# A fused retention and two-layer network kernel: V loads on SyncE's queue, each held for another load, and units 4 and 5 attended one by one

## The chip, the core and the metric

The kernel runs on one core of one Trainium2 chip. The metric is the device time of one execution in microseconds (us). The core has five engines with a queue each: PE (TensorE: matmuls, and PEld, its weight loads), DVE (VectorE), ACT (ScalarE), POOL (GpSimd) and SP (SyncE, which here only issues transfers). Transfers are issued by POOL, SP or ACT and carried out by 16 DMA engines that all of them share.

## The reference

Shapes: q, k and v are 8 x 8 x 576 x 64 (batch, heads, positions, head size). The first part is a retention with a decay per head, the second a two-layer network with a gated activation over 4608 tokens of 512 features:

```python
scores = scale * np.matmul(q, k.transpose(0, 1, 3, 2))
gamma = 1.0 - 2.0 ** (-5.0 - np.arange(H, dtype=np.float32))
Dmat = np.where(rel >= 0, gamma[:, None, None] ** rel[None, :, :], 0.0)
ret = np.matmul(scores * Dmat[None, :, :, :], v)
x = ret.transpose(0, 2, 1, 3).reshape(B * S, H * D)
h = x @ w_in                       # 512 -> 2048
g = h * (1.0 / (1.0 + np.exp(-1.702 * h)))
out = g @ w_out                    # 2048 -> 512
```

## The kernel before

**Tiles.** The 4608 tokens are 36 units of 128; four units are a chunk, so there are 9 chunks. A unit's attention ("scores", "values", "inter", "state" in the code) is made of matmuls of 64 x 64 blocks: `scores` (L632) multiplies K and Q, `scores_out` (L641, DVE) masks the result out of PSUM, `state_both` (L561) or `state_half` (L538) multiplies K and V to the running state, `state_sum` (L574, L576, DVE) adds it up, `state_cast` (L585, ACT) writes it as bf16 into `kv`, `values` (L654) multiplies masked scores and V, `inter` (L616) multiplies Q and the state before, and `x_out` or `x_out_pair` (L669, L679, DVE) takes the sum, scaled by the powers of gamma, to `xT`. V is first scaled to `vp` by `scale_v`: on DVE (L480) for units 0 to 7, on ACT (L476, eight instructions of 128x64 per unit) for units 8 to 13, on POOL (L480) for the others.

**The network.** The up projection of a chunk has 16 f tiles of 128 columns of w_in: `up` (L691) makes one f tile for all four units, `up_group` (L705) some f tiles for some of the units; each is followed by one GELU on ACT (L696, L710). From chunk 2 on, `UpSet` (L938, with L949, L953, L962) does the same with fewer products. The down projection is `Pair.run` (L815): seven products of 16 matmuls each, into PSUM banks A and B by turns, copied out by ACT (L828) or added by DVE (L831) into `osb`, and stored.

**Order.** `lead_in()` does units 0 to 3 one by one with parts of chunk 0's up projection, and with dummy matmuls (L1067, L1074) between. `chunk01()` (turn "early") does units 4 to 7, the f tiles 8 to 15 of chunk 0, chunk 1's up projection, and chunk 0's down projection. Units 4 and 5, and 6 and 7, are pairs there: `ahead(j)` gives scores and state of both units of pair j in one go, `block(j)` their values, inter and x. `steady()` runs chunk 1 (turn "first") to chunk 8. In its chunk 1, `hook(1)` calls `ahead(4)`: scores and states of units 8 and 9, between the second and the third product. So PE reaches that third product only when unit 8 and 9 have their scaled V and their transposes.

**Queues.** PE, POOL and SP execute in program order. ACT's and DVE's order is given by a table, PLACES: each operation of a stage has a number there, and the engine executes by 10000 times the turn plus that number, in order, waiting at each for what it needs. PADS gives, for each gap between stages or blocks, how many nops go into PE's instruction stream, one ahead of each of the next matmuls.

**Loads.** K and Q of unit u go to slot u % 12 of `kqn` (L352, L339, cast to bf16 on the way), V to slot u % 10 of `vn` (L365, kept in fp32); both by `load(u)`, all from POOL. Only K and Q of unit 0 are loaded by SP (L372), as fp32 into `osb`, and cast by DVE (L383). The order of POOL's queue in the lead-in: V0, unit 1, unit 2, w_in tiles 0 to 3 (two f tiles per `load_win`, each two DMAs, L387), unit 3, w_in 4 to 7, units 4 and 5, w_in 8 to 15, units 6 and 7, the four quarters of w_out (L394), units 8 and 9, then in `chunk01()` units 10 to 13. Units 0 to 7 are transposed on PE (L496, L491) and copied by ACT or DVE (L509, L512); units from 8 on by transposing DMAs from SP (`dma_transpose`, L526), the first of which waits for V of unit 13. Loads of units 14 to 17 wait for the transpose of unit 13 (`after`), those of later rounds for the transpose of the last unit of the round before. Chunk 0's outputs are stored from ACT's queue, the others from SP's.

Of the kernel before, what the change touches and what calls it, by code (L numbers as in the profile page):

```python
# [30 lines left out]
class Program:  # L31
# [121 lines left out]
    def emit(self, eng, handle, sems):  # L153
# [14 lines left out]


PLACES = {  # L170
    ("early", "dve"): (
# [4 lines left out]
    ),  # L176
    ("early", "act"): (
# [6 lines left out]
    ),  # L184
    ("first", "dve"): (
        -3094, -3087, -161, -1167, -3020, -1459, -1864, -375, -70, 0, 0, -35, 234, -24, 654, 1489, 1403,
        1276, 1426, 1691, 1817, 1256, 1747, 1826, 2319, 1955, 1955, 2266, 2319, 2279, 2367, 1889, 1921, 1958,
        2189, 2222, 2248,
    ),
    ("first", "act"): (  # L190
        89, 1405, 1317, 1538, 1564, 11282, 2193,
    ),
    ("second", "act"): (
        -7652, -7562, -5268, -5221, -6814, -6753, -5520, -5411, -4470, -3949, -4823, -1529, -4083, -3955,
        -1425, -2133, -3938, -3629, -2846, -2700, -1058, 1018, 139, 454, 1345, 2980, 1691, 2832, 13658, 4556,
    ),
    ("second", "dve"): (
# [3 lines left out]
    ),  # L201
    ("mid", "act"): (
        -5145, -5020, -1896, -1729, -4845, -3773, -3705, -1971, -1157, -678, -1349, 2396, -821, -802, 1635,
        2396, -223, 242, 412, 620, 2648, 2953, 2569, 2779, 3397, 4347, 3659, 3701, 13327, 4401,
    ),
    ("mid", "dve"): (
# [3 lines left out]
    ),  # L210
    ("last", "act"): (
        -5412, -4735, -4294, -4481, -4735, -4526, -4516, -4482, -4119, -3957, -4192, -2867, -4110, -4084,
        -2730, -2620, -3883, -3811, -3643, -3308, -2314, -1667, -2542, -1448, -1260, 3388, 5040, 7770, 5228,
        5609, 7636, 11553, 17449, 24766,
    ),
    ("last", "dve"): (
        -4089, -4052, -3782, -3778, -3506, -3367, -3219, -3202, -3136, -3108, -3104, -1962, -1838, -64, -245,
        5700, 171, 274, 5929, 7966, 3319, 9533, 11095, 16923, 5403, 9389, 20259, 16639, 2882, 7994, 13880,
        17309, 21551, 26523,
    ),  # L220
}
# [42 lines left out]
def bass_retnet_parallel__then__act_gelu_quick_kernel(  # L264
# [10 lines left out]
    with es:  # L275
# [93 lines left out]

        def load_kq0(which):  # L370
            src = (k, q)[which]
# [645 lines left out]
        def ahead(j):  # L1017
            if 2 * j < NU:
# [64 lines left out]
        def lead_in():  # L1083
            load_kq0(0)
            load_kq0(1)
            iota_small()
            iota_large()
            load_v(0)
            load(1)
            load(2)  # L1090
            load_win(0, 2)
            load_win(2, 2)
            load(3)
            load_win(4, 2)
# [12 lines left out]
            warm_quads(NQUAD)  # L1107
            warm(44, "A", 64)
# [70 lines left out]
            gq_next(5)  # L1179

        def chunk01():
            scale_v(4)
            transposes(4, "E", "D")
            transposes(5, "C", "K")
            scale_v(5)
            up(0, 8)
            ahead(2)
            now(ahead_out(2))
            for f in range(9, 12):
                up(0, f)  # L1190
            now(block(2, lambda: up(0, 12)))
            up(0, 13)
            for i in range(4):
                up_group(1, 2 * i, 2, 0, 2, "AB"[i % 2])
                if i == 1:
                    transposes(6, "E", "D")
                    scale_v(6)
            transposes(7, "C", "K")
            scale_v(7)
            up_group(1, 8, 2, 0, 2, "A")  # L1200
            ahead(3)
            now(ahead_out(3))
            up_group(1, 10, 2, 0, 2, "B")
            up(0, 14)
            up(0, 15)
            now(block(3, lambda: up_group(1, 12, 2, 0, 2, "A")))
            up_group(1, 14, 2, 0, 2, "B")
# [147 lines left out]
```

## Time and profile before

| what | us |
|---|---|
| median of 3 timed runs | 285.7 (285.69, 285.7, 289.03) |
| the profiled execution | 283.09 |
| its span in the trace | 281.3 |
| PE busy | 267.8 |
| DVE busy | 214.2 |
| ACT busy | 176.5 |
| POOL busy, of which until 50.8 us nearly without a gap | 135.3 |
| software (POOL) transfers, 22.82 MB, as a share of the 16 DMA engines' span | 71.9% |
| hardware (SP and ACT) transfers, 16.00 MB | 25.8% |
| lead-in: transposes of unit 4 start on PE | 24.7 |
| chunk 0's first down product starts on PE | 53.4 |
| chunk 1's third down product starts on PE | 71.8 |
| chunk 2's up projection starts on PE | 83.2 |

The stages overlap, since each engine has its own queue. The span is what the trace covers; the execution's own time is 1.8 us longer. Granted clock: 1.00 throughout. "Busy" of PE counts a matmul until its modelled end, so a small gap between two starts can be invisible in it; in this text a gap of PE is the time between two starts less what the same kind of matmul takes in an unbroken run.

### The profile page before, as it was taken

The numbers are of one execution on the slowest core, as the hardware profiler recorded it, in microseconds if no ns is written. First come the engines' busy times: TensorE is split into PE (matmuls) and PEld (weight loads), VectorE is DVE, ScalarE is ACT, GpSimd is POOL, SyncE is SP. The second block draws the span as 40 slices with busy tenths as digits, with TensorE's granted clock in tenths as the row PEclk, the third lists the DMA queues.
The fourth block names the chain that finished last, engine by engine and source line by source line (L and its number), as shares of the span: only waits on it lengthen the run. The fifth ranks groups of instructions, "written<-read, shape, count | busy, mean of one in ns | idle before, by whom it ended". The sixth has DMA issues, their size and how long they took to land.

```text
span 281.3 us, 10016 instructions
## 1 busy us (share of the span) xinstructions
PE 267.8 (95%) x4402; PEld 220.2 (78%) x4402; DVE 214.2 (76%) x418; ACT 176.5 (63%) x345; POOL 135.3 (48%) x167
## 2 busy tenths in 40 slices
PE   8898999999899999999999999998999999999895
PEld 6576487888688687878887888787878887888584
DVE  5764747878799699669886987796869887966671
ACT  7557675679527952894289428950894289428922
POOL 9999999200297249607755915680572020000000
PEclk9999999999999999999999999999999999999999
DMA  9999999989499979999998999894886070011013
GB/s 170 176 204 210 214 208 210 220 125 268 75 165 133 218 109 180 181 198 106 184 270 100 160 147 213 101 200 81 252 105 76 31 199 0 6 75 76 0 40 112
DMA packets 118027, 40.75 MB, mean 145 GB/s; under 512 B 104160, under 2 KB 111328, under 8 KB 117984
## 3 DMA queue, kind: packets, MB, share of 16 engines
q0 software_dynamic: 80800, 22.82, 71.9%
q1 hardware_dynamic: 36320, 16.00, 25.8%
q10 hardware_dynamic: 864, 1.31, 1.5%
q8 instruction: 34, 0.56, 0.8%
q14 instruction: 9, 0.07, 0.1%
HBM read 36.70 MB, written 9.44 MB: 164 GB/s over the span
## 4 chain that ended last, share of the span: by engine, by line
PE 65%; POOL 16%; ACT 8%; DMA 4%; DVE 3%; issue 2%; ACTq 0%; POOLq 0%
PE psB L815 18%; PE psA L815 14%; POOL kqn L352 7%; DMA vn<-in_v_dram 4%; POOL vn L365 4%; PE psA L938 4%; PE psK L938 4%; PE psX L938 4%; PE psC L938 4%; POOL w_in_sb L387 4%; ACT vp L476 3%; PE psE L938 3%; PE psD L938 3%; PE psY L938 3%; PE psB L938 3%; ACT gT L962 2%
## 5 line engine op out<-in xcount | busy, mean ns | idle before, releaser
L352 POOL DMA_DIRECT2D kqn<-in_k_dram x39 | 36.2, 936 | 49.8 <-DMA kqT<-kqn 49.8
L962 ACT ACTIVATE gT<-part 128x512 bf16<-128x512 f32 (+1 forms) x56 | 47.9, 878 | 0.6 <-DVE part L953 0.5
L828 ACT ACTIVATE osb<-psB 128x512 f32<-128x512 f32 (+1 forms) x25 | 14.7, 589 | 50.2 <-PE psB L815 50.2
L480 POOL TENSOR_TENSOR vp<-vn,vfac 128x512 bf16<-128x512 f32 x22 | 22.5, 1050 | 42.5 <-PE psD L938 35.4
L365 POOL DMA_DIRECT2D vn<-in_v_dram x40 | 37.9, 961 | 0.1
L352 POOL DMA_DIRECT2D kqn<-in_q_dram x37 | 34.4, 941 | 0.0
L815 PE MATMUL psB<-w_out_sb,gT 128*128 128x256 bf16 x224 | 27.0, 273 | 0.0
L815 PEld LDWEIGHTS psB<-w_out_sb,gT 128*128 128x128 bf16 x224 | 21.4, 98 | 4.2 <-DVE part L953 1.9
L585 ACT ACTIVATE kv<-stm 128x1024 bf16<-128x1024 f32 (+1 forms) x16 | 15.5, 970 | 4.3 <-DVE stm L576 4.3
L815 PE MATMUL psA<-w_out_sb,gT 128*128 128x256 bf16 x136 | 16.5, 273 | 1.2 <-ACT gT L962 1.2
L815 PE MATMUL psA<-wsum,part 128*128 128x256 bf16 x136 | 16.3, 273 | 1.4 <-ACT osb L828 1.4
L641 DVE TENSOR_TENSOR pm<-psC,mask 128x512 bf16<-128x512 f32 (+1 forms) x20 | 12.6, 632 | 5.8 <-PE psC L632 5.0
L815 PE MATMUL psB<-wsum,part 128*128 128x256 bf16 x136 | 16.4, 273 | 0.0
L815 PE MATMUL psA<-w_out_sb,part 128*128 128x256 bf16 x120 | 14.8, 273 | 1.5 <-issue 1.5
L815 PEld LDWEIGHTS psA<-wsum,part 128*128 128x128 bf16 x136 | 13.2, 98 | 3.0 <-ACT osb L828 1.5
L953 DVE TENSOR_TENSOR part<-psB,part 128x512 f32<-128x512 f32 x14 | 9.6, 686 | 7.8 <-ACT part L949 7.8
L815 PEld LDWEIGHTS psA<-w_out_sb,gT 128*128 128x128 bf16 x136 | 13.1, 98 | 3.0 <-ACT gT L962 1.5
L641 DVE TENSOR_TENSOR pm<-psD,mask 128x512 bf16<-128x512 f32 (+1 forms) x20 | 12.6, 631 | 3.7 <-PE psD L632 3.7
L679 DVE TENSOR_TENSOR xT<-psX,gq 128x512 bf16<-128x512 f32 x16 | 11.0, 686 | 5.2 <-PE psY L616 5.2
L815 PEld LDWEIGHTS psB<-wsum,part 128*128 128x128 bf16 x136 | 12.7, 98 | 1.9 <-issue 0.2
L476 ACT ACTIVATE vp<-vn,vfac 128x64 bf16<-128x64 f32 x48 | 12.5, 341 | 2.5 <-DMA vn<-in_v_dram 1.9
L815 PEld LDWEIGHTS psA<-w_out_sb,part 128*128 128x128 bf16 x120 | 11.2, 98 | 3.4 <-issue 1.9
(233 smaller groups left out, 772.0 us busy)
## 6 DMA issues: line engine op xcount, KB each, us to landing
vn<-in_v_dram POOLq DMA_DIRECT2D x32, 256.0 KB, 5.9
out_dram<-osb SPq DMA_DIRECT2D x26, 256.0 KB, 2.5
kqn<-in_k_dram POOLq DMA_DIRECT2D x31, 128.0 KB, 5.7
kqn<-in_q_dram POOLq DMA_DIRECT2D x31, 128.0 KB, 5.8
w_in_sb<-in_moe_w_in_dram POOLq DMA_DIRECT2D x16, 128.0 KB, 5.6
w_out_sb<-in_moe_w_out_dram POOLq DMA_DIRECT2D x4, 512.0 KB, 11.3
out_dram<-osb SPq DMA_DIRECT2D x10, 128.0 KB, 2.4
vn<-in_v_dram POOLq DMA_DIRECT2D x8, 128.0 KB, 7.0
```

Source lines behind the costliest of these rows:

```text
L352: e.dma_start(kqn[sl][p0 : p0 + n, which, :, :], src[b, :, s0 : s0 + n, :].rearrange("h p d -> p h d"),)
L365: e.dma_start(vn[sl][p0 : p0 + n, :, :], v[b, :, s0 : s0 + n, :].rearrange("h p d -> p h d"))
L387: op("pool", lambda e: [e.dma_start(w_in_sb[64 * pb : 64 * pb + 64, :, P * f0 : P * f0 + P * nf], moe_w_in[256 * pb : 256 * pb + 256, P * ...
L476: op("act", lambda e, h=h: e.activation(vp[u % NVP][:, h, :], vn[sl][:, h, :], AF.Copy, scale=vfac[:, ty, h : h + 1]), reads=[f"vn{sl}"] + ...
L480: op(eng, lambda e: e.tensor_tensor(vp[u % NVP].ap(), vn[sl].ap(), vfac[:, ty, :, None].to_broadcast([P, H, DH]), ALU.mult), reads=[f"vn{s ...
L585: op("act", lambda e: e.activation(kv[:, i0 % NKV : i0 % NKV + n, :, :], stm[:, i0 % 8 : i0 % 8 + n, :, :], AF.Copy), reads=[f"stm{(i0 + i ...
L641: op("dve", lambda e: e.tensor_tensor(pm[(u0 // 2) % 2][hh][:, c0:c1].rearrange("p (a i) -> p a i", i=64), ps32(SB[hh])[:, c0:c1].rearrang ...
L679: op("dve", lambda e: e.tensor_tensor(xT[ch % 2][:, slice(hh, 4, 2), P * jj : P * jj + 2 * P].rearrange("p g (u t) -> p u g t", u=2), ps32 ...
L815: op("pe", lambda e, x=x, y=y, t=t, s=not more and t == 0 and k == 0, z=k == NF // 2 - 1: e.matmul(bank[b][:, 256 * t : 256 * t + 256], x, ...
L828: op("act", lambda e: e.activation(dst[0], src[0], AF.Copy), reads=src[1], writes=dst[1])
L938: op("pe", lambda e, x=x, y=y, i=i, s=not more and i == 0 and k == 0, z=k == 1: e.matmul(bank[b][:, 256 * i : 256 * i + 256], x, y, start= ...
L962: op("act", lambda e: e.activation(dst, src, AF.Gelu_apprx_sigmoid), reads=reads, writes=[g_key(self.c, f0 + 2 * i + q, j) for i in range( ...
```

## The change

1. `load_v` issues from SP instead of POOL (all units), and in the first stages it is told to wait for another load: V0 and V1 for none, V2 for Q of unit 1, V3 for Q of unit 2, V4 for w_in tile 8, V5 for w_in tile 12, V6 for K of unit 5, V7 for K of unit 6, V8 for quarter 2 of w_out, V9 for K of unit 8, V10 to V13 for K of the unit before. Later V loads wait for the same transpose as before.
2. POOL's order in the lead-in: units 1 and 2, w_in 0 to 3, unit 3, w_in 4 to 11, unit 4, w_in 12 to 15, units 5 to 7, w_out, units 8 and 9 (K and Q alone).
3. Units 4 and 5 are done by a new `single(u)`, one at a time among the f tiles 8 to 15, instead of by `ahead(2)`; `block(2)` stays, with f tile 15 in its middle. Transposes of units 6 and 7 move ahead of chunk 1's up projection, whose groups are spread anew around `ahead(3)` and `block(3)`.
4. PLACES is on a scale ten times finer, with other numbers in every row, and so other orders on ACT and DVE; PADS has other numbers (574 nops for 324).

```diff
-        return 10000 * self.turn + (10 * n if row is None else row[n]), (self.turn, self.kind, n)
+        return 100000 * self.turn + (100 * n if row is None else row[n]), (self.turn, self.kind, n)
...
-    0, 0, 0, 0, 0, 0, 0, 24, 0, 0, 0, 30, 6, 0, 0, 78, 0, 0, 108, 0, 0, 78, 0, 0, 0,
+    0, 0, 92, 0, 0, 16, 16, 0, 0, 114, 0, 0, 99, 0, 0, 81, 0, 0, 104, 0, 0, 52, 0, 0, 0,
...
-        def load_v(u, after=(), eng="pool"):
+        def load_v(u, after=(), eng="sp"):
...
-            op(eng, f, reads=after, writes=[f"vn{sl}"], dma=f"d_vn{sl}_{eng}", ndma=len(unit_rows(u)))
+            op(eng, f, reads=after, writes=[f"vn{sl}"], dma=f"d_vn{sl}", ndma=len(unit_rows(u)))
...
+        def single(u):
+            pr.wide = False
+            scores(u)
+            state_both(u)
+            pr.wide = True
+            for hh in range(2):
+                scores_out(u, 1, hh)
+            for a in range(2):
+                state_sum(u, a)
...
+        def kq(u):
+            load_kq(u, 0)
+            load_kq(u, 1)
...
             load_kq0(0)
             load_kq0(1)
+            load_v(0)
+            load_v(1)
             iota_small()
             iota_large()
-            load_v(0)
-            load(1)
-            load(2)
+            kq(1)
+            kq(2)
+            load_v(2, after=["kq1_1"])
             load_win(0, 2)
             load_win(2, 2)
-            load(3)
-            load_win(4, 2)
-            load_win(6, 2)
-            load(4)
-            load(5)
-            for f in range(8, NF, 2):
+            load_v(3, after=["kq2_1"])
+            kq(3)
+            for f in (4, 6, 8, 10):
                 load_win(f, 2)
-            load(6)
-            load(7)
+            load_v(4, after=["win8"])
+            kq(4)
+            load_win(12, 2)
+            load_win(14, 2)
+            load_v(5, after=["win12"])
+            kq(5)
+            load_v(6, after=["kq5_0"])
+            kq(6)
+            load_v(7, after=["kq6_0"])
+            kq(7)
             for i in range(4):
                 load_wout(i)
             for u in range(8, 10):
-                load(u)
+                load_v(u, after=["wout2" if u == 8 else "kq8_0"])
+                kq(u)
...
         def chunk01():
+            up(0, 8)
+            up(0, 9)
+            transposes(4, "E", "D")
             scale_v(4)
-            transposes(4, "E", "D")
-            transposes(5, "C", "K")
+            up(0, 10)
+            single(4)
+            up(0, 11)
+            up(0, 12)
+            transposes(5, "E", "D")
             scale_v(5)
-            up(0, 8)
-            ahead(2)
-            now(ahead_out(2))
-            for f in range(9, 12):
-                up(0, f)
-            now(block(2, lambda: up(0, 12)))
             up(0, 13)
+            single(5)
+            state_cast(4, 6)
+            up(0, 14)
+            rest = block(2, lambda: up(0, 15))
+            transposes(6, "E", "D")
+            scale_v(6)
+            transposes(7, "C", "K")
+            scale_v(7)
+            now(rest)
...
             for u in range(10, 14):
-                load(u)
+                load_v(u, after=[f"kq{(u - 1) % NLD}_0"])
+                kq(u)
```

Of the orders that PLACES sets, one stretch is used in the prediction: ACT's scalings of V for units 8 to 13 (48 instructions) among chunk 0's last GELUs and the osb copies of chunk 0 and chunk 1. The numbers of some of them in the new row `("early", "act")`: the first three scalings (one each of units 9, 10 and 12) -8009, -4372 and -1504, the first osb copy of chunk 0 1593, unit 13's first scaling 16415, unit 8's last scaling 89452; chunk 1's first osb copy is at -42004 of the next turn, which is 57996 on this scale.

More of the change, by code (lines that the diff above doesn't have):

```diff
@@ L170 @@
 PLACES = {
-    ("early", "dve"): (
[4 rows of a table removed]
-    ),
-    ("early", "act"): (
[6 rows of a table removed]
+    ("early", "act"): (
[7 rows of a table added]
+    ),
+    ("early", "dve"): (
[5 rows of a table added]
     ),
     ("first", "dve"): (
-        -3094, -3087, -161, -1167, -3020, -1459, -1864, -375, -70, 0, 0, -35, 234, -24, 654, 1489, 1403,
-        1276, 1426, 1691, 1817, 1256, 1747, 1826, 2319, 1955, 1955, 2266, 2319, 2279, 2367, 1889, 1921, 1958,
-        2189, 2222, 2248,
+        -18210, -16914, 413, -2078, -18227, -9709, -3896, -8130, 104, 0, 0, 334, 10262, 7135, 6149, 14004,
+        20596, 13854, 15735, 20090, 20920, 13722, 20028, 21514, 37380, 22429, 23492, 34862, 37419, 34665,
+        38295, 27752, 22348, 24216, 24272, 27889, 32512,
@@ L189 @@
     ),
     ("first", "act"): (
-        89, 1405, 1317, 1538, 1564, 11282, 2193,
+        -42004, -6458, -8980, 5969, 9013, 80619, 33558,
     ),
     ("second", "act"): (
-        -7652, -7562, -5268, -5221, -6814, -6753, -5520, -5411, -4470, -3949, -4823, -1529, -4083, -3955,
-        -1425, -2133, -3938, -3629, -2846, -2700, -1058, 1018, 139, 454, 1345, 2980, 1691, 2832, 13658, 4556,
+        -87427, -82121, -75465, -63933, -77181, -76152, -68881, -68014, -59611, -51167, -61125, -38126,
+        -56531, -53981, -37403, -38405, -50929, -48020, -44894, -39488, -32958, -24931, -32905, -25744,
@@ L196 @@
+        -16823, 20858, -391, 30176, 128869, 64068,
     ),
     ("second", "dve"): (
[3 rows of a table removed]
[4 rows of a table added]
     ),
     ("mid", "act"): (
-        -5145, -5020, -1896, -1729, -4845, -3773, -3705, -1971, -1157, -678, -1349, 2396, -821, -802, 1635,
-        2396, -223, 242, 412, 620, 2648, 2953, 2569, 2779, 3397, 4347, 3659, 3701, 13327, 4401,
+        -57594, -51907, -17637, -18340, -27164, -24069, -23191, -20314, -13414, -6720, -15842, 10601, -9767,
+        -8496, 11385, 11863, -5143, -3589, 655, 8778, 17581, 22623, 12150, 21781, 27599, 39629, 30592, 35939,
@@ L205 @@
+        126126, 49988,
     ),
     ("mid", "dve"): (
[3 rows of a table removed]
[4 rows of a table added]
     ),
     ("last", "act"): (
-        -5412, -4735, -4294, -4481, -4735, -4526, -4516, -4482, -4119, -3957, -4192, -2867, -4110, -4084,
-        -2730, -2620, -3883, -3811, -3643, -3308, -2314, -1667, -2542, -1448, -1260, 3388, 5040, 7770, 5228,
-        5609, 7636, 11553, 17449, 24766,
[3 rows of a table added]
     ),
     ("last", "dve"): (
-        -4089, -4052, -3782, -3778, -3506, -3367, -3219, -3202, -3136, -3108, -3104, -1962, -1838, -64, -245,
-        5700, 171, 274, 5929, 7966, 3319, 9533, 11095, 16923, 5403, 9389, 20259, 16639, 2882, 7994, 13880,
@@ L219 @@
-        17309, 21551, 26523,
[3 rows of a table added]
     ),
@@ L1181, in chunk01 @@
         def chunk01():
+            up(0, 8)
+            up(0, 9)
+            transposes(4, "E", "D")
             scale_v(4)
-            transposes(4, "E", "D")
-            transposes(5, "C", "K")
-            scale_v(5)
-            up(0, 8)
-            ahead(2)
-            now(ahead_out(2))
-            for f in range(9, 12):
-                up(0, f)
-            now(block(2, lambda: up(0, 12)))
-            up(0, 13)
[L1193 to L1197, printed above, removed]
+            up(0, 10)
[3 more added lines that the diff above has]
+            transposes(5, "E", "D")
+            scale_v(5)
+            up(0, 13)
+            single(5)
[4 more added lines that the diff above has]
+            scale_v(6)
             transposes(7, "C", "K")
             scale_v(7)
-            up_group(1, 8, 2, 0, 2, "A")
+            now(rest)
+            for i in range(2):
+                up_group(1, 2 * i, 2, 0, 2, "AB"[i % 2])
             ahead(3)
             now(ahead_out(3))
[L1203 to L1207, printed above, removed]
+            for i in range(2, 4):
+                up_group(1, 2 * i, 2, 0, 2, "AB"[i % 2])
+            now(block(3, lambda: [up_group(1, 2 * i, 2, 0, 2, "AB"[i % 2]) for i in range(4, 6)]))
+            for i in range(6, 8):
+                up_group(1, 2 * i, 2, 0, 2, "AB"[i % 2])
             for i in range(8):
```

42 rows, old and new, of the table PLACES are left out of this document.

## The prediction

> **What bounds the kernel now.** I read the page's busy table, slices and chain first, then the stretches of ten microseconds, the chain of the stretch 42 to 72 us, the waits by stretch, the timelines of POOL and SP, and last the trace's landing record of each DMA.
>
> ```profile
> span 281.3 us, 10016 instructions
> PE 267.8 (95%) x4402; PEld 220.2 (78%) x4402; DVE 214.2 (76%) x418; ACT 176.5 (63%) x345; POOL 135.3 (48%) x167
> DMA  9999999989499979999998999894886070011013
> PE 65%; POOL 16%; ACT 8%; DMA 4%; DVE 3%; issue 2%; ACTq 0%; POOLq 0%
> ```
>
> TensorE is busy nearly throughout, so what can be won are its gaps and the dummy matmuls of the lead-in. Sixteen matmuls of 256 columns take 1.75 us; by that rate the starts of all matmuls leave 31 us in which PE does not stream: 13.4 us of it before 50 us, 2.9 us from 60 to 80 us, and 14.8 us after 80 us, there mostly a tenth at a time. The chain of the first 47 us is POOL issuing loads; the whole DMA row says that the engines of the transfers are full at the same time.
>
> ```profile
> 30.00:40.00 10.00, 9.59 (x158) 6.55 (x160) 4.45 (x8) 7.33 (x14) 10.00 (x15) 1.00 1.53 218
> 40.00:50.00 10.00, 9.32 (x181) 7.18 (x170) 7.79 (x19) 5.69 (x10) 10.00 (x13) 1.00 1.71 210
> 50.00:60.00 10.00, 10.00 (x94) 8.95 (x93) 7.03 (x19) 5.59 (x15) 0.82 (x1) 1.00 1.76 199
> 60.00:70.00 10.00, 9.69 (x118) 8.44 (x115) 8.96 (x14) 9.41 (x37) 0.00 (x0) 1.00 0.81 208
> ```
>
> The last three columns are clock, DMA share and GB/s, the fifth busy column is POOL. POOL stops at 50.8 us, and the transfers go on at 199 GB/s to 60: a backlog. The landing records give its pace: the 18 loads from K of unit 8 to V of unit 13 land one per 0.80 us (first of 16 increments 43.64 to 57.97 us), while POOL issues one per 0.88 us. A pair of w_in loads lands per 1.44 us against 1.23 us of issue, a w_out load per 2.57 us against 0.74.
>
> ```profile
> 46.94 11.63 DMA vn<-in_v_dram
> 58.59 0.35 ACT vp L476
> 61.40 3.56 ACT vp L476 x15
> 69.02 2.24 ACT vp L476 x9
> 71.26 0.49 ACT osb L828
> 71.79 0.28 PE psA L815
> ```
>
> This is the join that matters (start, length): V of unit 12 lands at 58.57 us, ACT works through the 48 scalings of units 8 to 13 (15 in 3.56 us, 0.24 us each) with its copies and GELUs, and the third product of chunk 1's first stage waits for it at 71.79 us.
>
> ```profile
> PE psA L691 <- DMA w_in_sb<-in_moe_w_in_dram: 1.1, 1, 1.1
> PE psA L815 <- ACT osb L828: 1.4, 1, 1.4
> PE psA L815 <- issue: 1.5, 2, 0.9
> 0.74 0.45 SPq L372 DMA_DIRECT2D osb<-in_k_dram  x1
> 1.25 0.57 SPq L372 DMA_DIRECT2D osb<-in_q_dram  x1
> 61.02 25.81 SPq L526 DMA_TRANSPOSE kqT<-kqn  x8
> ```
>
> The first wait is up(0, 8) on w_in tile 8 at 25.8 us, the second the join above, the third two gaps (108.8 and 193.1 us) in which PE waits for nothing the profile shows. SP, where V is put, issues two loads of just V's shape in 0.45 and 0.57 us and is then empty to 61 us.
>
> **V off POOL.** POOL loses 15 issues before 51 us, 15 x 0.88 = 13.2 us: its list would end at 38 us. Little of that is time of the transfers. With the landing paces, all loads up to unit 13 cost 28 x 0.8 + 13 x 0.8 + 8 x 1.44 + 4 x 2.57 = 54.6 us from the first packet at 1.9 us, so 56.5 us against the 57.97 seen. The Trainium skill, "DMA: Bandwidth & Descriptors", section "Issuing engines are not separate DMA queues", says the same as a rule: loads started by several engines run on the same 16 DMA engines, and only issue time is saved. By that rule alone the last V would come no earlier; what that gives here is the first rival below.
>
> On SP the issue costs 0.45 to 0.57 us, at most the 1.25 to 4 us that a transpose takes there under load. Behind the held V loads stand SP's transposes and stores. Up to unit 13 nothing else is due before 61 us. V of 14 to 17 (5 DMAs) waits for the transpose of 13 (lands 75.0) as POOL's did, in front of transposes 14 and 15, which wait for Q at 80.9 and 85.1 us anyway: hidden by 6 us. V of 18 to 21 is issued after 101.9, the next stores come at 116.2; later rounds have 127.8 and 139.7. If that cover of 10 us were gone, each held V would delay stores by its wait. POOL's scalings (L480) from 114 us wait for PE's psD, not for POOL; no gain there.
>
> **Lead-in, to 24.7 us.** V0 lands now at 7.99 us and V1 at 9.98, K1, Q1 at 8.55, 9.18. SP's own K0 and Q0 took 3.0 and 4.55 us from issue to last increment, so V0, issued at 1.85, comes at 4.9 to 6.4. K2 and Q2 (PE transposes at 11.4, 12.6) and w_in 0, 2 (up at 13.9, 15.3 just after they land at 13.85, 15.21) come two V issues earlier, 1.8 us by issue, less by the transfers. Waiting stays for DVE's and ACT's chain per unit. Between 0 and -2.0 us I take -1.3, the shift of V0's use (8.01 to about 6.7).
>
> **Units 4 and 5 one by one.** PE's instructions are the same in number. DVE's masks go from two 128x512 (0.69) to four 128x256 (0.42): +0.3 us, hidden while DVE is half idle (20 to 40 us: 9.7 of 20). Gone: the 1.1 us on w_in 8, now ahead of K4; the 0.4 us on x at 34 us. New: PE waits at the transposes of unit 5 for K5, Q5, now behind all eight w_in pairs, not four (about 0.5 us), for ACT's two copies of 0.48 us behind them (0.3), and for the kv cast (1.06 us) behind four sums of 0.42 (0.5, cover is tiles 14, 15). Net -0.2, between -1.5 and +1.5.
>
> **The join at 71.8 us takes most of this back.** ACT is in order, and the new list puts one scaling of unit 12 (key -1504) ahead of the first osb copy (1593). From V12's landing L, 44 scalings (0.24), 5 osb copies (0.49) and 4 GELUs (0.49) stand up to unit 8's last scaling: 10.4 + 2.4 + 2.0 = 14.8 us, and then 0.2 us of state matmuls. The third product starts at L + 15.0, whatever PE had won before. Break-even is L = 56.8. V12 is held for K11, which landed at 54.58; the start-up gives 1.0 back, and a V load no longer waiting in POOL's ring something. K11 at 52.3 to 54, plus 3.0 to 4.55 us as for K0, Q0: L = 55.3 to 58.5. I take 55.4, near the lower end, since by then SP's ring is empty. So the third product starts at 70.4: -1.4 us, and the -1.5 of the two parts before is the same time and is not added. Bounds -4.5 (ACT not binding: PE alone loses its 2.0 us of stalls here, 0.9 at 44.7, and 1.6 from above) to +1.7.
>
> **Orders and pads after that.** Nops go from 324 to 574. They cost nothing visible: PE's up stages with 0, 78 and 108 nops all take 12.58 us from first to last start. They move where the 16,384-byte instruction packets (34 of them on the instruction queue, about 1 us each) fall: at 193.1 us PE resumes just as one that began at 192.03 is in. Gaps to win: 0.34 (84.8), 0.75 (91.3, ACT late), 0.72 (108.8), 1.10 (193.1), sum 2.9. I take half and a bit, -1.6; bounds -2.9 to +2 (two new ones). The Trainium skill, "Runtime: NRT & Kernel Launch", section "Instruction fetch mechanics", holds the crossing of a 16 KiB boundary mostly hidden. Most of the 34 here are. By it the pads would be worth nothing, the sum would be -1.4 and the time 284.3 us, inside the forecast's own range.
>
> **Sum.** The profiled execution took 283.09 us (span 281.3, 1.8 around it). -1.4 - 1.6 = -3.0 gives 280.1. The median shown, 285.7, is 2.6 above that execution; 282.7 beside the median.
>
> **Rivals.**
> - *The join does not move* (0.11): the transfers are full, V12 lands at 56.8, pads change nothing. For: 199 GB/s after POOL has stopped. Against: V12 goes ahead of K12 and Q12, 1.6 us of transfers. The transfers' sum, 56.5, is 1.5 us under the 57.97 seen; half of that reaches the join: 285.0. The two sections of the Trainium skill named above point to this case.
> - *ACT is no longer last* (0.32): V on its own queue lands by 52.3, the PE gains all count: -4.5 and -2.9, so 278.3. For: loads issued by SP have 18 ns packets against 36 to 40 ns for POOL's; against: both run on full engines.
> - *V12 late holds ACT, slower* (0.13): the scaling of unit 12 blocks the first osb copy, PE waits for bank and copy. Price: one for one from L = 56.8 on. With L as now, 58.57, +1.8; with the longest landing seen for a V, 12.7 us after K11 at 53, L = 65.7 and +8.9: 287.5 to 294.6. For: ACT waited 1.9 us on this very load before. Against: 10 of those 12.7 us were POOL's backlog.
>
> **How the numbers follow.** The forecast, 0.44: 282.7, own range 280.5 to 284.5. 2% of 285.7 is 5.7 us, about what a measurement of this kernel can tell from no change. Faster: the second rival and 0.03 of the forecast, 0.35. Slower: 0.09, the third where L passes 62.5. Same: 0.56. The range 277.0 to 288.0 holds the forecast, the first two rivals and the third up to +2.
>
> **What would show it.** Right: POOL's list ends near 38 us, V0 at DVE before 7 us, no wait on w_in 8, V12 near 55.4, third product near 70.4, transfers still full to 57 us. Wrong: K or Q landing later than now because V shares the engines, a wait at unit 5's transposes over 1.5 us, SP late with stores at 89.6 us, or new unexplained PE gaps after 100 us.

## The result and the profile after

| | before | changed kernel |
|---|---|---|
| median, us | 286.23 (285.69 to 289.03) | 310.58 (305.62 to 312.53) |
| ratio to before | | 1.0714, 95% interval 1.0557 to 1.087 |
| profiled execution, us | 283.09 | 312.27 |
| its span, us | 281.3 | 310.5 |
| V of unit 12 landed, us | 58.57 | 69.94 |
| chunk 0's first down product starts, us | 53.44 | 67.73 |
| chunk 1's third down product starts, us | 71.80 | 84.28 |
| chunk 2's up projection starts, us | 83.19 | 101.22 |

The changed kernel is 7% slower: the forecast of 282.7 and its range up to 288.0 are both missed. The profiled execution is one of the longer of its four runs; the ratio leaves the two longest out. Of the 29.2 us of span, 14.3 are lost up to chunk 0's first down product, 12.5 up to chunk 1's third product (the kernel before had a wait of its own there), 18.0 up to chunk 2's start, and 11 more behind it.

From the page of the changed kernel: span, busy time of the engines, TensorE's and the granted clock's slices, the DMA share, and the chain that ended last by engine.

```profile
span 310.5 us, 10010 instructions
PE 278.0 (90%) x4396; PEld 225.1 (72%) x4402; DVE 214.7 (69%) x420; ACT 176.4 (57%) x345; POOL 101.2 (33%) x127
PE   7689692999987999699999949999899999999986
PEclk9779976899997999999999977999999999999999
DMA  9999999998899079929999892589968815003003
PE 67%; DMA 12%; POOL 10%; issue 5%; ACT 4%; POOLq 0%; SPq 0%
```

POOL did get shorter, 135.3 to 101.2 us, and its share of the chain fell from 16% to 10%. In its place stands DMA, 4% to 12%, and "issue" went from 2% to 5%. Those two are the two losses of this case: the first in the first 70 us, the second in TensorE's gaps (4 to 6 in the PE row) later on.

The stretches of ten microseconds of the changed kernel from 40 to 70 us (columns as in the prediction's: PE, PEld, DVE, ACT, POOL, then clock, DMA share, GB/s):

```profile
40.00:50.00 10.00, 5.86 (x108) 3.75 (x107) 1.29 (x2) 5.01 (x9) 0.00 (x0) 0.84 1.27 194
50.00:60.00 10.00, 7.72 (x138) 5.85 (x139) 5.29 (x11) 3.23 (x5) 0.00 (x0) 0.68 1.97 157
60.00:70.00 10.00, 10.00 (x94) 8.97 (x92) 9.54 (x25) 3.88 (x9) 0.00 (x0) 1.00 1.44 157
```

POOL is empty from 38.65 us on and the transfers are as busy as before (1.97 in 50 to 60 us, 1.76 before), but they move 157 GB/s where they moved 199. So the same bytes take longer, and the backlog that ended at 60 us now ends at 71. DVE, 7.79 us busy of the stretch 40 to 50 before, is busy for 1.29.

The clock, 1.00 in every stretch before, is 0.66 from 10 to 20 us, 0.96 from 30 to 40, and 0.84 and 0.68 in the first two lines above. The waits of the changed kernel up to 110 us say for what DVE, and behind it PE, stood still (us in total, times, longest):

```profile
DVE vp L486 <- DMA vn<-in_v_dram: 19.4, 6, 7.1
PE psK L567 <- DVE vp L486: 8.0, 3, 6.1
ACT vp L482 <- DMA vn<-in_v_dram: 3.5, 1, 3.5
```

DVE scales V of units 0 to 7 (L486) and waits for V itself; PE's state matmuls of units 6 and 7 (L567) wait for DVE, the gap of 6.3 us at 46.0 us. V of unit 7 ends it: it lands at 50.90 us, where it landed at 36.51 before, and the first down product is late by as much, 14.3 us. Behind it the chain of the same kernel, from the stretch 25 to 100 us (start, length):

```profile
26.41 6.02 POOL kqn L358 x8
32.43 29.60 DMA kqn<-in_k_dram
...
62.09 7.84 DMA vn<-in_v_dram
69.96 0.35 ACT vp L482
...
74.39 0.50 ACT osb L834
74.88 0.05 issue
74.93 1.92 PE psB L821 x16
76.85 1.75 PE psA L821 x16
78.60 1.75 PE psB L821 x16
80.34 1.75 PE psA L821 x16
82.09 1.75 PE psB L821 x16
83.84 0.14 PE psC L638
...
84.34 1.85 PE psA L821 x16
```

K of unit 11, issued at 32.4 us, lands 29.6 us later; V of unit 12, which is held for it, takes another 7.84 us; then comes ACT's stretch up to 74.9. There the chain passes from ACT to PE, but by a hair: PE has run without a break from its first down product at 67.73, waits 0.3 us for this copy, and runs on to the third product. By PE's own work that product would have come 0.3 us earlier.

What the transfers are made of is in the page's queue lines (packets, MB, share of 16 engines' span) and its list of issues (KB each, median us from issue to landing). Before:

```profile
DMA packets 118027, 40.75 MB, mean 145 GB/s; under 512 B 104160, under 2 KB 111328, under 8 KB 117984
q0 software_dynamic: 80800, 22.82, 71.9%
q1 hardware_dynamic: 36320, 16.00, 25.8%
vn<-in_v_dram POOLq DMA_DIRECT2D x32, 256.0 KB, 5.9
w_out_sb<-in_moe_w_out_dram POOLq DMA_DIRECT2D x4, 512.0 KB, 11.3
```

And of the changed kernel:

```profile
DMA packets 152587, 40.75 MB, mean 131 GB/s; under 512 B 141024, under 2 KB 148192, under 8 KB 152544
q0 software_dynamic: 77856, 13.38, 54.7%
q1 hardware_dynamic: 73824, 25.44, 41.0%
vn<-in_v_dram SPq DMA_DIRECT2D x32, 256.0 KB, 7.5
w_out_sb<-in_moe_w_out_dram POOLq DMA_DIRECT2D x4, 512.0 KB, 23.2
```

The bytes are the same, 40.75 MB, the packets 34,560 more. In the trace's packet records V from POOL is 64 packets of 4,096 bytes per unit (2,304 in all, 172 ns each at the median; the 32 ns packets of 128 bytes on POOL's queue are K and Q); V from SP is 1,024 packets of 256 bytes per unit (36,864 in all, 18 ns alone, about 31 ns beside POOL's). That is one packet per run of 64 fp32 values, where POOL's hold sixteen such runs.

### The profile page after: what moved, and what is told of

Read it like the earlier page. It is cut to its first block, busy times and chain, and to the rows that moved or that the text cites. A ratio compares the mean times of both kernels' runs of the same rounds, so it can differ in the third digit from the quotient of the medians.

```text
span 310.5 us, 10010 instructions
## 1 busy us (share of the span) xinstructions
PE 278.0 (90%) x4396; PEld 225.1 (72%) x4402; DVE 214.7 (69%) x420; ACT 176.4 (57%) x345; POOL 101.2 (33%) x127
## 2 busy tenths in 40 slices
DMA packets 152587, 40.75 MB, mean 131 GB/s; under 512 B 141024, under 2 KB 148192, under 8 KB 152544
## 4 chain that ended last, share of the span: by engine, by line
PE 67%; DMA 12%; POOL 10%; issue 5%; ACT 4%; POOLq 0%; SPq 0%
PE psB L821 18%; PE psA L821 15%; DMA kqn<-in_k_dram 10%; POOL kqn L358 5%; PE psX L944 4%; PE psC L944 4%; PE psA L944 4%; PE psK L944 4%; POOL w_in_sb L393 3%; PE psD L944 3%; PE psY L944 3%; PE psE L944 3%; PE psB L944 3%; DMA vn<-in_v_dram 3%; ACT gT L968 2%
## 5 line engine op out<-in xcount | busy, mean ns | idle before, releaser
L486 POOL TENSOR_TENSOR vp<-vn,vfac 128x512 bf16<-128x512 f32 x22 | 22.3, 1035 | 78.7 <-PE psD L944 78.7
L968 ACT ACTIVATE gT<-part 128x512 bf16<-128x512 f32 (+1 forms) x56 | 47.1, 875 | 0.0
L955 ACT ACTIVATE part<-psX 128x512 f32<-128x512 f32 x14 | 8.4, 597 | 47.5 <-PE psX L944 47.5
L358 POOL DMA_DIRECT2D kqn<-in_q_dram x37 | 33.5, 915 | 0.0
L486 DVE TENSOR_TENSOR vp<-vn,vfac 128x512 bf16<-128x512 f32 x8 | 5.4, 691 | 19.4 <-DMA vn<-in_v_dram 19.4
L821 PE MATMUL psB<-wsum,part 128*128 128x256 bf16 x136 | 18.1, 290 | 0.0
L821 PE MATMUL psA<-wsum,part 128*128 128x256 bf16 x136 | 17.2, 281 | 0.0
L482 ACT ACTIVATE vp<-vn,vfac 128x64 bf16<-128x64 f32 x48 | 12.5, 339 | 5.4 <-DMA vn<-in_v_dram 3.5
L821 PEld LDWEIGHTS psB<-wsum,part 128*128 128x128 bf16 x136 | 13.5, 103 | 2.6 <-DVE part L802 0.2
L685 DVE TENSOR_TENSOR xT<-psY,gq 128x512 bf16<-128x512 f32 x16 | 10.9, 684 | 5.8 <-PE psY L622 5.8
L567 PE MATMUL psK<-vp,kqn 64*64 64x64 bf16 x224 | 7.3, 201 | 8.0 <-DVE vp L486 8.0
## 6 DMA issues: line engine op xcount, KB each, us to landing
w_in_sb<-in_moe_w_in_dram POOLq DMA_DIRECT2D x16, 128.0 KB, 10.7
```

Source lines behind the costliest of these rows:

```text
L358: e.dma_start(kqn[sl][p0 : p0 + n, which, :, :], src[b, :, s0 : s0 + n, :].rearrange("h p d -> p h d"),)
L482: op("act", lambda e, h=h: e.activation(vp[u % NVP][:, h, :], vn[sl][:, h, :], AF.Copy, scale=vfac[:, ty, h : h + 1]), reads=[f"vn{sl}"] + ...
L486: op(eng, lambda e: e.tensor_tensor(vp[u % NVP].ap(), vn[sl].ap(), vfac[:, ty, :, None].to_broadcast([P, H, DH]), ALU.mult), reads=[f"vn{s ...
L685: op("dve", lambda e: e.tensor_tensor(xT[ch % 2][:, slice(hh, 4, 2), P * jj : P * jj + 2 * P].rearrange("p g (u t) -> p u g t", u=2), ps32 ...
L821: op("pe", lambda e, x=x, y=y, t=t, s=not more and t == 0 and k == 0, z=k == NF // 2 - 1: e.matmul(bank[b][:, 256 * t : 256 * t + 256], x, ...
L955: op("act", lambda e: e.activation(d, bank[b].ap(), AF.Copy), reads=[b], writes=kd)
```

## The experiments

"SP" and "POOL" below say which queue issues V. All variants keep the rest of the changed kernel unless it is said otherwise. Theory A: V from SP costs more transfer time and takes turns with POOL's loads, because of its small packets. Theory B: the one-by-one units, the orders and the pads cost the time. Theory C: the holds make V late, or SP's queue costs something whatever its packets are. Theory D, which the first runs led to: in the later rounds, loads of both queues in flight delay PE's instruction packets.

### Which part of the change: three runs

v_pool puts all of V back on POOL, without the holds of the first stages (this and the variants that use both queues have a semaphore of V's slot for each queue):

```diff
         def load_v(u, after=(), eng="sp"):
+            eng, after = "pool", (after if u >= 14 else ())
```

> The changed kernel with every V load issued by POOL at its place in the program and without holds before unit 14; units 4 and 5 one by one, orders and pads as changed. Theory A (V on SP is cut into 256-byte packets, 36,864 of them for 2,304 of 4,096 bytes, and costs the DMA engines more): the first down product starts at 52 to 56 us (67.7 in the changed kernel, 53.4 before), V of unit 13 lands at 58 to 62 us, time 283 to 291. Theory B (units one by one, the new orders): the first down product stays after 62 us and the time over 300.

Measured: 285.12 us, ratio 1.0007 (0.9966 to 1.0048). The third product of chunk 1 starts at 71.28 us, chunk 2 at 82.88. Everything but V's queue and holds together is worth nothing that this interval shows, in either direction; theory B falls.

v_pool_early leaves V of units 14 and up on SP, v_pool_late V of units 0 to 13 (with its holds):

```diff
+            eng, after = ("sp", after) if u >= 14 else ("pool", ())     # v_pool_early
+            eng = "pool" if u >= 14 else "sp"                           # v_pool_late
```

> V of units 0 to 13 from POOL without holds, of 14 to 35 from SP as changed. Theory A: the first 70 us as with all V on POOL, so 13 to 15 us are won. What is left over that kernel is the cost of V on SP in the later rounds: if PE's gaps after 88 us (1.7, 2.5, 1.9, 1.8, 4.8 us) are instruction packets held up by V's packets, 6 to 12 us; if they come from the new pads, under 2 us. Theory B: over 300.

Measured: 294.51 us, ratio 1.0319 (1.0203 to 1.0435), 9.4 us over v_pool. Chunk 1's third product starts at 71.90 us, so nearly all of it comes later, most of it in gaps of PE; the largest is at 162.2 us.

> V of units 0 to 13 from SP with their holds, of 14 to 35 from POOL. Theory A: the first down product still starts at 66 to 69 us; the later gaps go if they come from V's packets (time 295 to 301), and stay if they come from the pads (305 to 312). Theory B: as the changed kernel, 305 to 312.

Measured: 297.08 us, ratio 1.0412 (1.0254 to 1.057), 12.0 us over v_pool. Here the third product starts at 84.36 us, as in the changed kernel, and from there on nothing more is lost. The wait list of v_pool_late up to 75 us has the changed kernel's first line again:

```profile
DVE vp L487 <- DMA vn<-in_v_dram: 16.0, 4, 9.1
```

The two halves add up: 285.1 + 9.4 + 12.0 = 306.5 us, inside the 305.6 to 312.5 of the changed kernel. There are two losses, and they have to be explained apart. The early one is not made at the join: v_pool executes the same PE program, and against it the changed kernel is 14.3 us late at the first down product and 13.0 us at the third product of chunk 1.

### The early loss: holds or packets

no_hold keeps V on SP and takes the holds of units 0 to 13 away:

```diff
+            after = after if u >= 14 else ()
```

> The changed kernel with V of units 0 to 13 on SP without the holds (each waits for its slot alone). Theory A (packets cost the DMA engines more): V comes early, K and w_in come late instead, the first down product still starts after 60 us (53.4 with V on POOL, 67.7 with holds), time 298 to 312. Theory C (the holds release V too late, the queue costs nothing): first down product at 53 to 57 us, time 290 to 298, as with V on POOL in the early part.

Measured: 310.07 us median (304.79 to 311.77), before 285.57 in the same set; no interval comes with it. The first down product starts at 66.71 us (67.73 with the holds). The holds, the first half of theory C, fall as the cause: without them V is early, unit 12's lands at 48.33 us and unit 13's at 55.99 (58.57 and 60.93 before), and POOL's loads are late in its place. Q of unit 7 lands at 50.71 (35.77 before), the last quarter of w_out at 60.98 (46.71), and Q of unit 13, the last of all, at 75.97 (60.17). The holds only choose which load pays.

b_v_sp is the kernel before with one word changed, nothing else of the change:

```diff
-        def load_v(u, after=(), eng="pool"):
+        def load_v(u, after=(), eng="sp"):
```

> The kernel before with V alone moved to SP, no holds; units in pairs, orders and pads as before. Theory A: slower by most of what the whole change costs, 295 to 310. Theory B (units one by one, orders): 284 to 290.

Measured: 306.23 us median (301.58 to 307.07), no interval, first down product at 66.39 us. The queue alone costs 16 to 21 us. V is early here too (unit 12's at 51.76 us); PE's longest waits are for a scaled V of the lead-in (2.8 us), w_in and Q (2.0 each).

v_runs keeps V on SP with its holds, but reads V in runs of 1,024 bytes, so that a unit is 256 packets. To do so it puts V's heads and positions in other places of the tile; bytes, waits and all later work are the same.

```diff
-                    e.dma_start(vn[sl][p0 : p0 + n, :, :], v[b, :, s0 : s0 + n, :].rearrange("h p d -> p h d"))
+                    e.dma_start(
+                        vn[sl][p0 : p0 + n, :, :].rearrange("p (g h) d -> p g (h d)", g=2),
+                        v[b, :, s0 : s0 + n, :].rearrange("h (p t) d -> p h (t d)", t=4))
```

> The changed kernel with every V load on SP, held as changed, but read in runs of 1,024 bytes instead of 256 (the rows of a unit come in another order, so the output is not the reference's; the bytes and the instructions are the same). Theory A: a V has 256 packets of 1,024 bytes instead of 1,024 of 256, the engine time of a V load falls from 64 x 18 to 16 x 46 ns, from 1.15 to 0.74 us, and V's share of the turns beside POOL's packets rises: first down product at 54 to 60 us, the PE gaps over 1.5 us in the later rounds mostly gone, time 284 to 294. Theory C (holds or SP's queue as such): as the changed kernel, over 302.

Measured: 301.3 us, ratio 1.0504 (1.0392 to 1.0616), 7 us over what theory A expected and just under theory C's 302. But the early part is as theory A has it: V of unit 13 lands at 61.23 us (before 60.93, changed kernel 70.98) and the first down product starts at 55.32. From the page of v_runs:

```profile
DMA packets 124939, 40.75 MB, mean 136 GB/s; under 512 B 104160, under 2 KB 120544, under 8 KB 124896
vn<-in_v_dram SPq DMA_DIRECT2D x32, 256.0 KB, 6.5
w_out_sb<-in_moe_w_out_dram POOLq DMA_DIRECT2D x4, 512.0 KB, 17.9
```

V of units 6 and 7, the second of which held up PE in the changed kernel, land 3.9 and 2.1 us after the V before each, where it was 7.9 and 5.6 us. So the size of the packets makes most of the early loss (12.4 of 14.3 us at the first down product). What is left of the 301.3 lies behind it, in gaps of PE: 2.3 us at 58.7, where PE waits for ACT's osb copy, then 2.2, 1.5, 1.5, 4.0 and 2.6 us in which it waits for no engine and no load. The late loss isn't packet size.

### The loads by themselves

Three kernels replace the program's stages by bare loads, in phases that wait for each other; everything that computes is left out.

```diff
-        lead_in()
-        pr.stage("early")
-        chunk01()
-        steady()
+        loads_only()     # per phase: 8 V and/or 8 K loads, or 4 quarters of w_out, on a given queue
```

> No matmuls, no network, only loads in phases that wait for each other (the output is not the reference's): 8 V from POOL, 8 V from SP, 8 K from POOL, 8 V from SP beside 8 K from POOL, the same 16 all from POOL, 8 V from SP in runs of 1,024 bytes, the 4 quarters of w_out beside 4 V from SP, the same all from POOL, and w_out alone. Theory A: per V load 0.7 to 0.9 us from POOL, 1.0 to 1.3 from SP in 256-byte packets and under 0.9 in runs; K beside V on SP takes 20% longer in all than all from POOL; beside w_out a V from SP lands 10 us or more after its issue. Rival (transfers cost the same from either queue, only order matters): the pairs of phases differ by under 5%.

In loads_only SP's loads, and all loads of the mixed phases, each waited for the one before, so it gave single loads alone: from issue to last landing about 3.4 us for V from POOL and 3.0 from SP. It says nothing of loads beside each other.

> Loads only, in phases that wait for each other, within a phase back to back (the earlier kernel waited between single loads too; the output is not the reference's). Theory A, us per load in the middle of a phase: V from POOL 0.85 to 0.9 (POOL's issue sets it), V from SP 1.1 to 1.3, V from SP in 1,024-byte runs 0.7 to 0.9; 8 V from SP beside 8 K from POOL 17 to 20 us in all against 14 to 15 all from POOL; 4 V from SP beside w_out: the last V over 9 us after its issue, against under 4 alone. Rival (either queue costs the same): V from SP 0.85 or less, both mixed phases within 5%.

In loads_phases V from SP and K again hardly overlapped. From the second of eight loads to the last, a load landed every 0.86 us for V from POOL, 0.98 for V from SP, 0.91 for K from POOL: alone, the queue makes little difference, less than theory A's 1.1 to 1.3 for SP. The one V from SP that ran beside w_out landed 10.1 us after its issue.

> Loads only, phases that wait for each other, back to back within each (the output is not the reference's): 8 V POOL; 8 V SP; 8 K POOL; 8 V SP in 1,024-byte runs beside 8 K POOL; 8 V SP in 256-byte runs beside 8 K POOL; the same 16 all from POOL; V SP in runs; w_out beside 4 V SP; w_out and 4 V from POOL; w_out. The two kernels before it did not run K beside V. Theory A: the 16 loads take 13 to 15 us from the first landing to the last all from POOL (0.81 to 0.87 us each), 16 to 20 with V from SP in 256-byte runs, 12 to 15 in 1,024-byte runs. Rival (K and V from two queues simply overlap): under 13 in both SP phases.

loads_beside has the overlap. Sixteen loads, 8 V and 8 K by turns, from first issue to last landing:

| V from | K from | us |
|---|---|---|
| POOL | POOL | 17.5 |
| SP, 256-byte runs | POOL | 20.3 |
| SP, 1,024-byte runs | POOL | 16.8 |
| SP, alone | none | 10.8 |
| POOL, alone | none | 10.9 |
| none | POOL, alone | 10.7 |

By the expectation's measure, from the first landing to the last, the three mixed rows are 14.0, 17.4 and 13.5 us, all inside theory A's ranges; each is one execution. Two queues with small packets are slower than one queue with everything, by (20.3 - 17.5) / 8 = 0.35 us per V, and with 1,024-byte runs they are not. Beside w_out, the last two of four V from SP took 14.1 and 17.2 us to land, and a quarter of w_out 3.35 us where it takes 2.6 alone. That is the changed kernel again, whose quarters land every 3.35 us (2.57 before). Theory A holds. By these rows 14 V loads cost 14 x 0.35 = 4.9 us and four quarters 3.0, together 7.9 of the 10.05 us by which V of unit 13 is later; the rest stays unassigned. This counts the transfers' end, at 71 us. PE's loss is settled before it, by V of unit 7, which is 14.4 us later than before because it stands behind V of unit 6 on SP's queue while w_out moves.

### The late loss

In the chain of v_pool_early at its largest gap (start, length), PE is in chunk 4's down stage, between two matmuls of the same kind:

```profile
162.22 0.03 PE psX L623
162.26 0.03 PE psX L623
162.41 3.50 issue
165.91 0.21 PE psX L623
```

No engine and no load is waited for. In the records of the instruction queue a packet of 16,384 bytes runs from 163.46 to 164.34 us, and PE resumes at 165.9, some 1.6 us after its end. In v_pool the same packet runs from 157.20 to 158.09 and the gap at the same matmuls is 1.37 us: there the packet starts 1.2 us before PE runs dry, here 1.1 us after. From 155 to 167 us v_pool_early has five V loads from SP in flight beside ten of K and Q from POOL; v_pool has the same loads there, all from POOL. So late_after_kq starts from v_pool_early and issues a round's V only when the round's last Q has landed, with the same queue, the same packets, the same bytes (and later in time):

```diff
-                for u in range(4 * c + 10, 4 * c + 14):
-                    load(u, after=[f"T{(4 * c + 9) % NQT}_0"])
+                us = [u for u in range(4 * c + 10, 4 * c + 14) if u < NU]
+                for u in us:
+                    load_kq(u, 0, after=[f"T{(4 * c + 9) % NQT}_0"])
+                    load_kq(u, 1, after=[f"T{(4 * c + 9) % NQT}_0"])
+                for u in us:
+                    load_v(u, after=[f"kq{us[-1] % NLD}_1"])
```

> V of units 0 to 13 from POOL, V of 14 to 35 from SP, but issued only when the last Q of its round has landed, so that SP's and POOL's loads are hardly in flight together. Theory D (PE's gaps in the later rounds are instruction packets standing in line behind both queues' loads): the gap of 3.7 us near 162 us falls to 1.6 or less, and the time from 294.5 to 284 to 289. Rival (V on SP is late for its scaling, or SP's order is what costs): 292 or more.

Measured: 283.89 us (282.99 to 284.58), ratio 0.9936 (0.9906 to 0.9967). The 9.4 us are gone. The same place in its chain:

```profile
158.23 0.03 PE psX L623
158.37 1.32 issue
159.69 0.21 PE psX L623
```

The packet is back at 157.20 to 158.26 us. At this place the gap is 0.99 to 1.5 us in the four kernels whose V isn't beside POOL's loads (v_pool, v_pool_old_pads, v_pool_late, late_after_kq) and 2.9 to 4.8 us in the five where it is (b_v_sp, v_pool_early, v_runs, no_hold, changed kernel). Theory D holds as far as the overlap goes: with it the packet comes late, without it it doesn't. Of the 9.1 us between the spans of v_pool_early and late_after_kq, 5.8 are waits put down to "issue" (9.1 against 3.3 us from 70 us on), and the clock, 0.85 from 160 to 170 us and 0.98 behind it, makes 1.7 more at the most; the rest stays open. The sheer number of loads in flight is a rival, since as this gap opens v_pool has four and v_pool_early eight. One place speaks against it: at 44.7 us of the kernel before, with sixteen loads of POOL in flight and none of SP's, the gap is 0.7 us. One gap doesn't fit theory D: that of 2.6 us in v_runs at 210.1, where the last V has landed at 205.6. late_after_kq is also the version that beats both kernels, by 0.6% over the one before.

The last two runs test the pads. v_pool_old_pads is v_pool with the PADS of before, before_new_pads the kernel before with the new PADS:

```diff
-    0, 0, 92, 0, 0, 16, 16, 0, 0, 114, 0, 0, 99, 0, 0, 81, 0, 0, 104, 0, 0, 52, 0, 0, 0,
+    0, 0, 0, 0, 0, 0, 0, 24, 0, 0, 0, 30, 6, 0, 0, 78, 0, 0, 108, 0, 0, 78, 0, 0, 0,
```

> All V from POOL, units 4 and 5 one by one and the new orders, with the pads of the kernel before. If the new pads suit this instruction stream, as forecast (1.6 us won): 286 to 288 against 285.1. If where the gaps fall is chance: 283 to 287 with other gaps than at 108.5 and 158.3 us.

Measured: 284.37 us, ratio 0.9963 (0.9926 to 1.0), with gaps of 1.1 at 108.7, 1.0 at 158.0 and 1.5 at 194.6 us.

> The kernel before with the new pads alone. If pads only move the gaps: 284 to 288, gaps at other places than 108.8 and 193.1 us. If the pads are good for either stream: 283.5 to 285, with one of the two gaps gone.

Measured: 287.39 us, ratio 1.0019 (0.9983 to 1.0055). The gap at 193.1 us is gone, and new ones of 1.7 and 0.8 us stand at 88.6 and 112.5. The pads move the gaps about and win nothing that can be measured.

## Why the prediction was wrong, step by step

**"V off POOL" failed, and with it the forecast.** The step charged each V 0.80 us from either queue and saw only POOL's issue time change. (Its sum has 13 V loads where units 0 to 13 are 14; with 14 it gives 57.3 us, nearer to the 57.97 seen.) Its one look at packets compared the time of one (18 ns against 36 to 40), not how many a load is made of. From packet records of the kernel before, where SP's K and Q of unit 0 are already 1,024 packets of 256 bytes each, the price could have been bounded, as an estimate: 64 packets x 172 ns / 16 engines = 0.69 us from POOL, 1,024 x 18 / 16 = 1.15 us from SP, up to 1,024 x 31 / 16 = 1.98 us beside POOL's. Measured in the kernel is (70.98 - 60.93) / 14 = 0.72 us more per V, and 1.075 us per load in the stretch from K of unit 8 to V of unit 13 in place of 0.80. POOL's list did end as said, at 38.65 us (forecast 38): the issue was saved, the transfers had no room for the price. What PE lost by it is a wait that the sum put at nothing: for the scaled V of units 5 to 7.

The Trainium skill, "DMA: Bandwidth & Descriptors", section "Queues, rings and completion order", says that a DMA engine goes round its queues and drains a whole packet of one before it takes the next queue. The trace fits it: V of unit 6 lands 7.9 us after V of unit 5 while w_out is moving, and 64 packets per engine that each let one w_out packet of 98 ns go ahead make, as an estimate, 64 x (18 + 98) to 64 x (31 + 98) ns, 7.4 to 8.3 us. By the same count 16 packets of 59 ns make 16 x (59 + 98) ns = 2.5 us, and in v_runs, with its 1,024-byte packets, V of units 6 and 7 land 3.9 and 2.1 us after the one before.

**Lead-in.** V0 was to land at 4.9 to 6.4 us and landed at 9.06 (7.99 before); -1.3 us became a gap of 2.6 us at 7.1 us (1.2 before at 7.5). In v_pool, where V0 is POOL's first load, it lands at 5.46.

**Units 4 and 5** came out as said as far as v_pool shows it: the 1.1 us on w_in tile 8 is gone, and with V on POOL and the old pads the kernel is at 0.9963 (0.9926 to 1.0), about -1.1 us. That interval reaches 1.0, and the figure holds the new orders and POOL's new list as well. In the changed kernel PE waits for the scaled V of unit 5 (1.8 us) and of unit 7 (6.3 us). Neither wait is costed in any step; these, and the lowered clock behind them, are what the early loss is made of.

**The join** did not decide, and its formula comes out by luck. V of unit 12 landed at 69.94, plus 15.0 gives 84.9, measured 84.28. But PE waited only 0.3 us for ACT there, and the third product came when it did because PE had been running without a break since 67.73. Unit 8's last scaling, on which the formula lets that product wait, starts at 86.98 us, 2.7 us after it. Unit 8 needs none so early: `state_both` does nothing for every ninth unit, so of the pair 8 and 9 only unit 9 has a state product between the second and the third product, and V of unit 8 is first used by `values` at 87.9. (The text ahead of the prediction has this wrong too.) So "whatever PE had won before" fails: what PE had lost before set the time. The landing L was wrong in both its terms: K of unit 11 was to land at 52.3 to 54 and landed at 62.03, and V after it was to take 3.0 to 4.55 us and took 7.84. The third rival, "V12 late holds ACT, slower", had the sign and 0.13, but not the path: ACT did wait 3.5 us for V of unit 12, and it cost PE 0.3. Its longest landing, 12.7 us, was that of a V in POOL's ring; V of unit 7, which did cost PE, took 16.7.

**"Hidden" for the later V loads** asked only whether stores and transposes behind them on SP have time, and PE waits for none of them. It didn't ask what else uses the DMA engines at that moment: PE's own instructions. That is most of the 9.4 us of v_pool_early.

**Pads, -1.6 us:** not seen (0.9983 to 1.0055). The packets were the right thing to look at, but the step misread its example: the packet that began at 192.03 us is in at 193.08, where PE stops, and PE resumes 1.2 us later, at 194.32. And when a packet starts, against PE's own progress, changed with the loads in flight, which nops don't touch. The wait list of the changed kernel from 110 us on, where the prediction feared "new unexplained PE gaps":

```profile
PE psX L622 <- issue: 4.6, 1, 4.6
PE psA L821 <- issue: 2.4, 2, 1.7
PE psB L821 <- issue: 1.7, 1, 1.7
```

The Trainium skill, "Runtime: NRT & Kernel Launch", section "Instruction fetch mechanics", calls the crossing of a 16 KiB boundary mostly hidden. Most are hidden here too; but a late packet costs 0.7 to 1.8 us with loads of POOL alone in flight (2.6 once), and 1.2 to 4.8 us with loads of both queues.

## What to carry to other kernels

Before a load is moved to another queue, count its packets in the trace on both queues, not only its bytes and its issue time: where the DMA engines are full, more packets are a price and a second queue is a second claimant, and PE, which waited in order for the scaled V of one unit, passed that price on: V of unit 7 came 14.4 us later and the first down product 14.3. A hold doesn't remove the price, it chooses the load that pays it. In a steady phase, try to keep loads of two queues from being in flight together while an engine with a long instruction stream is due for its next packet; here it was enough to issue one queue's loads after the other's had landed. A wait put down to "issue" at one and the same instruction in every variant is worth a look at the instruction queue's packets. And a formula that hits a time isn't confirmed until the trace shows that the thing it names was waited for.

## What the runs showed of the hardware that was not expected

- The same load with runs of 256 bytes is 64 packets of 4,096 bytes from POOL and 1,024 packets of 256 bytes from SP. Alone both take the same time (eight in 10.9 and 10.8 us); with eight K from POOL beside them, all sixteen loads take 17.5 and 20.3.
- PE resumes 1.2 to 1.6 us after the end of a late instruction packet, in all gaps of over 0.8 us behind 80 us that are put down to "issue", in eleven traces, but one (0.95 us, at 88.6 us of before_new_pads). What holds the packet back when both queues have loads in flight (its start at 181.68 us in the changed kernel, 2.4 us after PE's last start) stays open; that the long gap goes away when V waits for Q is shown.
- Gaps of PE cost a second time, in the granted clock. The stretch of the changed kernel with the 4.8 us gap, third figure from the end:

```profile
180.00:190.00 10.00, 5.91 (x32) 4.29 (x33) 4.78 (x10) 0.60 (x1) 1.18 (x2) 0.66 1.48 115
```

Before, with no gap over 1.6 us, every stretch shows 1.00; after the 3.5 us gap of v_pool_early its stretch shows 0.85. Not every gap is followed by it: after those of 1.9 and 1.8 us from 123 to 130 us of the changed kernel the clock stays at 1.00. The clock's share of the early loss isn't measured apart from the waits, and it was in no term of the sum.
